# Linear attention's output product: the last two heads' numerators taken through the zero rows of the other heads

## The chip, the cores and the metric

One core of one Trainium2 chip. The metric is the device time of one execution in microseconds; the runs shown give its median. All data is float32; the matrix products of the large stages run in fp32r on operands split into a high and a low half, so that one product of the mathematics is three on the engine (high by high, high by low, low by high).

## The reference, cut to what matters

```python
def _A_ref(x, wqkv, w_phi, wo):          # S = 2048 tokens, D = 640, H = 32 heads of 20
    q, k, v = ...                          # x @ wqkv, by head
    phi_q = concat([softmax(q @ w_phi), softmax(-(q @ w_phi))])   # 40 features a head
    phi_k = ...                            # the same of k
    kv = einsum("bhsf,bhsd->bhfd", phi_k, v)
    z = einsum("bhsf->bhf", phi_k)
    num = einsum("bhqf,bhfd->bhqd", phi_q, kv)
    den = einsum("bhqf,bhf->bhq", phi_q, z)[..., None] + 1e-6
    return (num / den).reshape(B, S, D) @ wo

h = layernorm(x) * (1 + ca) + sa           # sa, ca, ga, sb, cb, gb: six rows made from c
x = x + ga * _A_ref(h, ...)
h = layernorm(x) * (1 + cb) + sb
x = x + gb * (relu(h @ w1 + b1) ** 2 @ w2 + b2)
```

## The kernel before, in words

The tokens are worked in 16 tiles of 128, two tiles a pair `j` (0 to 7). The program has three stretches: K, V and Q with the sums over all tokens; then the division, the numerators and the output product; then the feed-forward part. Only the middle one is touched. There the engines' orders are written out by hand (`manual_schedule`): each of TensorE (PE), VectorE (DVE), ScalarE (ACT) and GpSimd (POOL) takes its instructions as the Python code issues them. SP's order, which holds most loads, comes from a scheduler. The loop `for j in range(NB)` at line 1188 makes eight passes; pass `j` finishes the output product of pair `j` and prepares the numerators of pair `j + 1`.

Names that the text uses:

- 32 heads of 20 are six groups: five of 120 columns (six heads) and a sixth of 40 (the last two heads, called the tail here). `kvd` holds K-by-V of the five as 120 features by two halves of 64 columns, of which 60 are the head columns and 4 are zero; `kv5` holds the tail's, 80 by 40, three times beside each other.
- `e_prod`, `e_recip`, `e_scale` (DVE and POOL, lines 877 to 914): denominators, and the exponentials `ezb` scaled by them.
- `tr_e(j, gs)` (line 916): TensorE transposes `ezb` into a bank `te`, ACT copies the bank to `ept` (lines 927 and 929). The banks `te`, `numa` and `numb` come in turn from three buffers, the six `ept` of a pair from five.
- `num(j)` (line 931): for each of the five groups two fp32 products, 64 columns each, beside each other in the array, to `numa`, `numb` and the first half of `numc`; the tail's two products (64 and 56 columns: its 40 rows three times) go to the second half of `numc`.
- `num_hi` and `num_lo` (lines 952 and 956): ACT copies a high half to `ot`; DVE subtracts to the low half (`lo`, line 89). For pairs 0 and 1 the subtraction is a product with the negated identity, and ACT copies the low half.
- `do_wo(j, i, h)` (line 972): the output product of token tile `2j + i`, half `h` of the columns (384 or 256): 15 products for the five groups and a 16th for the tail, whose three kinds stand in one 120-row operand; then ACT copies `pwo` to `at`, and after the second half a DMA on ACT's queue stores `at` to `a1`.
- `plus_x(j)`: POOL's accumulating DMAs add x to `a1`.
- `prep_wo(g)` (line 489): loads the rows of `wo` for a group into `rwo`, 60 to each half, the four rows between set to zero, and splits them.
- `p_load`, `p_hi`, `p_lo` (lines 992 to 1049): the feed-forward weights, loaded by SP into `rw` or `rawt` and split by ACT and DVE into `w`.

Of the kernel before, what the change touches and what calls it, by code (L numbers as in the profile page):

```python
# [11 lines left out]
AF = mybir.ActivationFunctionType  # L12
# [3 lines left out]
P = 128  # L16
# [21 lines left out]
PLAIN = 2  # L38
DEALT = range(NT // 2)
DIRECT = 2  # L40
LAST = 3
W_AT = (
    *range(21),
# [9 lines left out]
def kernel(  # L53
# [67 lines left out]
    def feat(tag, name):  # L121
        return row(tag, name)[:, :512].rearrange("p (s n) -> p s n", s=2)
# [366 lines left out]
    def prep_wo(g, ga_b):  # L489
        o, n = GR[g]  # L490
        t = row("s1", f"rwo{g}")
        m = P
        if g < 5:
            nc.gpsimd.memset(t, 0.0)
            for c in range(2):
                nc.sync.dma_start(t[64 * c : 64 * c + 60], wo[o + 60 * c : o + 60 * c + 60])
        else:
            m = 3 * n
            for i in range(3):
                nc.sync.dma_start(t[i * n : i * n + n], wo[o : o + n])  # L500
        w = wslot(f"wo{g}")
        WO[g] = w
        with tc.issue_after(newest(ET_.DVE)):
            nc.vector.tensor_tensor(t[:m], t[:m], ga_b[:m], op=ALU.mult)
        nc.scalar.activation(w[:m, 0], t[:m], AF.Copy)
        lo(w[:m, 1], t[:m], w[:m, 0])
        if g == 5:
            nc.gpsimd.dma_start(w[2 * n : m, 0], w[2 * n : m, 1])
# [303 lines left out]
    zb = tok2("w", "zb")  # L812
    kvtile = tok2("w", "kvd")
    kv_t = flat(kvtile)
    kvd = kv_t[:120, :640].rearrange("p (g n) -> p g n", n=P)
    kv5 = kv_t[:80, 640:760]
    def make_z():
        at = [(c, b) for b in range(2) for c in range(2)]
        ps = {}
        for c, b in at:  # L820
            r, a, n = slice(64 * c, 64 * c + 64), 480 * b, ((480, 200), (480, 120))[c][b]
            p = ps[c, b] = tp("z") if len(ps) == 3 else bank(f"z{c}_{b}")
            nc.tensor.matmul(p[:, :n], ident[r, 64 * c + 60 : 64 * c + 61].to_broadcast([64, P]),
                             kvs[r, a : a + n], start=True, stop=True)
# [75 lines left out]
    def e_scale(t):  # L900
# [12 lines left out]
            dn[:, :, 30:, None].to_broadcast([P, 2, 2, DH]), op=ALU.mult  # L913
        )

    def tr_e(j, gs):
        for g in gs:
            o, n = GR[g]
            p = bank(f"te{j}_{g}")
            t = EPT[j, g] = feat("s4", f"ept{j}_{g}")  # L920
            for i in range(2):
                for c in range(2 if g < 5 else 1):
                    a = c * 256 + i * P
                    b, m = (2 * o + 120 * c, 120) if g < 5 else (1200, 80)
                    nc.tensor.transpose(p[:m, a : a + P], EU[2 * j + i][:, b : b + m], ident)
            if g < 5:
                nc.scalar.activation(t[:120], p[:120].rearrange("p (s n) -> p s n", s=2), AF.Copy)
            else:
                nc.scalar.activation(t[:80, 0], p[:80, :256], AF.Copy)

    def num(j):
        OT[j] = ht(f"ot{j}", j)
        ps = [bank(f"numa{j}"), bank(f"numb{j}"), tp(f"numc{j}")]
        for g in range(5):
            for c in range(2):
                mm(ps[g // 2][64 * c : 64 * c + 64, (g % 2) * 256 : (g % 2) * 256 + 256],
                   [(kvd[:, g, 64 * c : 64 * c + 64], EPT[j, g][:120, c])], first=(g % 2 == 0), last=False, skip=True)
        for a, b in ((0, 64), (64, 120)):
            mm(ps[2][a:b, 256:], [(kv5[:, a:b], EPT[j, 5][:80, 0])], first=False, last=False, skip=True)
        NUM[j] = ps  # L940
        OT[j, 5] = row("s3", f"ot5_{j}")[:, 80:336].bitcast(F32R)

    NUM = {}
# [1 line left out]
    def num_parts(j):  # L945
        ps, parts = NUM[j], []
        for b, g in ((0, 2), (1, 2), (2, 1)):
            t = OT[j][:, 2 * b : 2 * b + g]
            parts.append((ps[b][:, : 256 * g].rearrange("p (g n) -> p g n", n=256), t[:, :, 0], t[:, :, 1]))
        return parts + [(ps[2][:120, 256:], OT[j, 5][:120], OT[j, 5][:120])]  # L950

    def num_hi(j):
        for src, hi, _ in num_parts(j):
# [15 lines left out]

    PWO, AT = {}, {}  # L970

    def do_wo(j, i, h, a=0, b=16):
        t = 2 * j + i
        if h == 0 and a == 0:
            PWO[t] = pj(f"pwo{t}")
            AT[t] = row("s2", f"at{t}")
        s = slice(i * P, (i + 1) * P)
        cs_, n = slice(*CUT[h]), CUT[h][1] - CUT[h][0]
        terms = []
        for g in range(5):  # L980
            w, o = WO[g], OT[j]
            terms += three(o[:, g, 0, s], o[:, g, 1, s], w[:, 0, cs_], w[:, 1, cs_])
        terms.append((OT[j, 5][:120, s], WO[5][:120, 0, cs_]))
        mm(PWO[t][h][:, :n], terms[a:b], first=(a == 0), last=(b == 16))
        if b == 16:
            nc.scalar.activation(AT[t][:, cs_], PWO[t][h][:, :n], AF.Copy)
            if h:
                nc.scalar.dma_start(A1[t], AT[t])
# [199 lines left out]
    for j in range(NB):  # L1188
        nxt = j + 1 < NB
        b, c = 2 * j + 5, 2 * j + 6  # L1190
        te_at = (0, 1) if 0 < j < 6 else (1, 2)
        if j == 4:
            load_x1(0)
            load_dealt(0)
        if j < 5:
            p_load()
        if j != 5:
            e_prod(b)
        e_recip(b - 1)
        e_scale(b - 1)  # L1200
        if j == 6:
            mod_sum(5, gate_b)
        if j == 5:
            q_chain(KEPT + 3, False)
        load_e(b + 2)
        def te(at):
            for i, gs in enumerate((range(3), (3, 4, 5) if te_at[0] == 0 else (5, 3, 4))):
                if nxt and te_at[i] == at:
                    tr_e(j + 1, gs)

        do_wo(j, 0, 0)
        te(0)
        if j == 5:
            exps(EQ[KEPT + 3])
            q_sums(KEPT + 3)
            e_prod(b)
        do_wo(j, 0, 1)
        if j == 7:
            t2(0, 0)
            t2(0, 1)  # L1220
        te(1)
        if j == 4:
            ln0 = ln_dealt(0)
            next(ln0)
            next(ln0)
        if j == 6:
            next(ln0)
            turn(0, 0)
            turn(0, 1)
        if j == 2:  # L1230
            exps(EQ[KEPT + 1])
        if j in SUMS:
            q_sums(KEPT + SUMS[j])
        e_prod(c)
        if j != 5:
            e_recip(b)
            e_scale(b)
        do_wo(j, 1, 0)
        if j == 7:
            t2(0, 2)  # L1240
            t2(0, 3)
        te(2)
        if nxt:
            num(j + 1)
            num_hi(j + 1)
        do_wo(j, 1, 1, 0, 8)
        if j == 7:
            t2(0, 4)
            p = tp("gbt")[:NC, :P]
            nc.tensor.transpose(p, gate_b, ident)  # L1250
            nc.scalar.activation(gate_r, p, AF.Copy)
            nc.sync.dma_start(GD[1], gate_r)
            nc.sync.dma_start(gb_b, GD[1].rearrange("c p -> (c p)")[None, :].to_broadcast([P, D]))
        if not nxt:
            do_wo(j, 1, 1, 8, 16)
        if nxt:
            do_wo(j, 1, 1, 8, 11)
            num_lo(j + 1)
            do_wo(j, 1, 1, 11, 16)
# [12 lines left out]
        if j == 4:  # L1272
            next(ln0)
            next(ln0)
            next(ln0)
        if j == 5:
            next(ln0)
        if j == 5:
            p_lo(4)
            p_load(4)  # L1280
        if j == 6:
            p_hi(4)
            p_lo(5)
            p_load(3)
        if j == 7:
            p_load(2)
# [485 lines left out]
```

## Time and profile before

| | |
|---|---|
| median of 3 runs | 756.28 us (756.26 to 756.48) |
| span of the profiled execution, first to last instruction | 754.9 us |
| TensorE busy, granted clock | 749.6 us (99%), 1.000 |
| VectorE, ScalarE, GpSimd busy | 607.5, 458.8, 170.4 us |
| HBM read and written | 100.94 and 29.89 MB |

The profile is of one execution; its times are counted from its first instruction. The profiled execution has no time of its own beside the span; the runs' median is 1.4 us above it. Busy times of TensorE count pipelined products with modelled ends, so a busy engine can still be late. A row of a timeline is: start, us, engine, line, operation, output and input, count, and in brackets the idle time ahead with what ended it. In a chain a row is: start, us, engine, tile, line, count. "ACTq" and "SPq" are the engines' queues issuing DMAs. The middle stretch lies at about 266 to 389 us.

### The profile page before, as it was taken

To read this page: it belongs to the slowest core of one execution; us is meant where nothing else is said; L and a number is where in the kernel's file an instruction comes from. 1 tells how busy PE (TensorE), PEld (TensorE's weight loads), DVE (VectorE), ACT (ScalarE), POOL (GpSimd) and SP (SyncE) were. 2 spreads that over 40 slices of the span, in tenths; PEclk is the share of its full clock that TensorE was granted. 3 is DMA by queue.
4 is the path that set the end of the run, shared out by engine and by line. 5 is a ranking of instruction groups with operands and counts; after the bars stand their busy time and mean duration, and the time that the engine had idled before them with its cause. 6 is when DMAs were issued, how large, how long until landed. Compare 5 with 4: busy or idle time off the path is not lost.

```text
span 754.9 us, 15404 instructions
## 1 busy us (share of the span) xinstructions
PE 749.6 (99%) x5888; PEld 731.9 (97%) x5888; DVE 607.5 (80%) x1123; ACT 458.8 (61%) x1060; POOL 170.4 (23%) x365
## 2 busy tenths in 40 slices
PE   9999999999999999999999999999999999999998
PEld 9999999999999998998899999999999999999997
DVE  6598987988999899999755768787777776777766
ACT  5767666677863355556677757485574756647431
POOL 3001101011200237646303030132221313213110
PEclk9999999999999999999999999999999999999999
DMA  9811431342432264664777475897677767667461
GB/s 324 336 39 80 155 96 70 106 139 103 138 105 93 71 190 142 143 153 124 173 204 218 121 216 215 278 326 204 185 213 204 205 196 212 191 181 208 132 188 36
DMA packets 58931, 126.70 MB, mean 168 GB/s; under 512 B 7452, under 2 KB 16417, under 8 KB 58857
## 3 DMA queue, kind: packets, MB, share of 16 engines
q1 hardware_dynamic: 38706, 79.41, 32.1%
q0 software_dynamic: 17568, 41.00, 22.0%
q10 hardware_dynamic: 2583, 5.30, 1.9%
q8 instruction: 46, 0.75, 0.5%
q14 instruction: 28, 0.23, 0.1%
HBM read 100.94 MB, written 29.89 MB: 173 GB/s over the span
## 4 chain that ended last, share of the span: by engine, by line
PE 86%; DVE 11%; POOL 1%; issue 1%; ACT 0%; DVEq 0%; POOLq 0%
PE up L79 24%; PE acc L79 18%; PE pk L79 9%; PE pv L79 9%; PE pq L79 8%; PE acc3x L79 5%; PE pwo L79 3%; PE kvp L455 3%; DVE dn L883 3%; DVE scr L881 2%; DVE ezb L905 2%; PE foldk L281 1%; PE ta L363 1%; DVE ot L89 1%; POOL dn L889 1%; PE foldq L281 1%
## 5 line engine op out<-in xcount | busy, mean ns | idle before, releaser
L79 PE MATMUL up<-h,w 128*128 128x256 f32 x1640 | 204.4, 276 | 0.1
L79 PEld LDWEIGHTS up<-h,w 128*128 128x128 f32 x1640 | 196.4, 188 | 0.5 <-DVE h L89 0.3
L1321 ACT ACTIVATE ft<-up,b_t 128x256 f32<-128x256 f32 x104 | 48.9, 471 | 96.0 <-PE up L79 95.6
L79 PE MATMUL acc<-w,ra 128*128 128x384 f32 x452 | 97.5, 335 | 0.0
L79 PE MATMUL pwo<-wo,ot 128*128 128x256 f32 (+3 forms) x512 | 79.9, 311 | 0.4 <-DVE ot L89 0.4
L1322 DVE TENSOR_TENSOR ft<-ft 128x256 f32<-128x256 f32 x104 | 43.8, 421 | 43.0 <-ACT ft L1321 41.4
L79 PEld LDWEIGHTS pwo<-wo,ot 128*128 128x128 f32 (+1 forms) x512 | 74.3, 188 | 3.5 <-issue 2.7
L79 PE MATMUL pq<-wq,hT 128*128 128x384 f32 (+1 forms) x480 | 75.1, 311 | 0.0
L79 PEld LDWEIGHTS acc<-w,ra 128*128 128x128 f32 x452 | 72.7, 188 | 0.9 <-DVE ra L89 0.6
L79 PE MATMUL pk<-wk,hT 128*128 128x384 f32 (+1 forms) x480 | 72.7, 308 | 0.0
L79 PE MATMUL pv<-wv,hT 128*128 128x384 f32 (+1 forms) x480 | 71.6, 306 | 0.0
L79 PEld LDWEIGHTS pq<-wq,hT 128*128 128x128 f32 x480 | 71.0, 188 | 0.6 <-issue 0.2
L79 PEld LDWEIGHTS pk<-wk,hT 128*128 128x128 f32 x480 | 70.5, 188 | 0.4 <-issue 0.2
L79 PEld LDWEIGHTS pv<-wv,hT 128*128 128x128 f32 x480 | 70.0, 188 | 0.0
L89 DVE TENSOR_TENSOR ra<-ft,ra 128x384 fp32r<-128x384 f32 (+2 forms) x86 | 36.8, 449 | 32.7 <-ACT ra L1345 19.4
L1431 POOL DMA_DIRECT2D ring_a<-td_a x34 | 18.5, 544 | 117.1 <-PE acc L79 103.7
L1345 ACT ACTIVATE ra<-ft 128x384 fp32r<-128x384 f32 x48 | 25.2, 526 | 28.5 <-DVE ft L1322 22.4
L79 PE MATMUL acc3x<-w,ra 128*128 128x256 f32 x231 | 39.5, 278 | 0.0
L79 PEld LDWEIGHTS acc3x<-w,ra 128*128 128x128 f32 x231 | 37.2, 188 | 0.0
L1336 DVE TENSOR_TENSOR ft<-ft 128x128 f32<-128x128 f32 x136 | 33.4, 286 | 1.2
L446 DVE TENSOR_REDUCE sk<-ek 128x64 f32<-128x1280 f32 x16 | 23.7, 1483 | 12.4 <-ACT ek L441 10.8
L889 POOL TENSOR_TENSOR dn<-dn,rs_q 128x32 f32<-128x32 f32 x32 | 19.9, 622 | 59.0 <-DVE dn L883 58.7
(264 smaller groups left out, 1458.2 us busy)
## 6 DMA issues: line engine op xcount, KB each, us to landing
ring_c<-td_c POOLq DMA_DIRECT2D x34, 384.0 KB, 4.1
ring_a<-td_a POOLq DMA_DIRECT2D x34, 384.0 KB, 3.5
ring_b<-td_b POOLq DMA_DIRECT2D x34, 256.0 KB, 3.5
esp<-eq SPq DMA_DIRECT2D x12, 640.0 KB, 3.2
el<-esp SPq DMA_DIRECT2D x12, 640.0 KB, 4.4
rw<-in_w SPq DMA_DIRECT2D x23, 320.0 KB, 3.5
wm<-in_w_mod SPq DMA_DIRECT2D x20, 320.0 KB, 3.7
xb<-in_x SPq DMA_DIRECT2D x8, 640.0 KB, 4.0
```

The lines of the kernel that those rows point to most:

```text
L79: nc.tensor.matmul(o, a, b, start=first and i == 0, stop=last and i == len(terms) - 1, skip_group_check=skip,)
L89: (eng or nc.vector).tensor_tensor(out_lo, full, hi.bitcast(F32), op=ALU.subtract)
L281: nc.tensor.matmul(p[g // 3][:, (g % 3) * 120 : (g % 3) * 120 + n], r, bd_t[:120, g * 120 : g * 120 + n], start=True, stop=True,)
L446: nc.vector.tensor_reduce(s, heads(flat(e)), axis=AX.X, op=ALU.add)
L455: nc.tensor.matmul(kvp[g // 4][64 * c : 64 * c + 64, a : a + 2 * n].rearrange("p (s n) -> p s n", s=2), v[:, u], e[:, :, o : o + n], start ...
L883: nc.vector.tensor_reduce(dn.rearrange("p s h -> p (s h)"), heads(z), axis=AX.X, op=ALU.add)
L889: nc.gpsimd.tensor_tensor(dn[:, s], dn[:, s], rs[:, 1 - s], op=ALU.mult)
L1321: nc.scalar.activation(r, p, AF.Relu, bias=b1_t[:, f : f + 1])
L1322: nc.vector.tensor_tensor(r, r, r, op=ALU.mult)
L1336: nc.vector.tensor_tensor(t[:, o], t[:, a], t[:, b], op=op)
L1345: nc.scalar.activation(a[:, 0, :3], t[:, :3], AF.Copy)
L1431: nc.gpsimd.dma_start(RING[j, n, r], TD[n][r].bitcast(F32R))
```

## The change

From pair 1 on (`JOINED = 1`) the tail has no rows of its own in `ot`. `kvd` gets eight more rows, 120 to 127, which hold ones so that row 120 + 4c + r goes to column 60 + r of half c of each group. `ept` of the five groups gets eight rows of the tail's numerators in its partitions 120 to 127, and the 128-row products of `num` write them to the four columns of each half that were zero. `wo`'s rows 600 to 639 are loaded to the matching rows of the five `rwo` tiles, which POOL no longer clears.

To have the tail's numerators early, `num_tail` does them by one 40-column product ahead of `num`, in the middle of a half of `do_wo`: behind 8 of the 15 products of (0, 1) in passes 1 to 5, behind 6 of (1, 0) in passes 0 and 6. ACT copies them out of `numc`, and five DMAs on ACT's queue bring eight rows each, once for each half, to the five `ept`. For that the sixth group is transposed first: `tr_e` takes groups 5, 0, 1 and then 2, 3, 4, where it took 0, 1, 2 and then 3, 4, 5 (5, 3, 4 in passes 0 and 6). `do_wo` of pairs 1 to 7 has 15 products, `num` 10 where it had 12, and the tail's high and low half go from ACT and DVE. Pair 0 is as before, with the tail's 16th product.

```diff
+JOINED = 1
...
 def prep_wo(g, ga_b):
-            nc.gpsimd.memset(t, 0.0)
             for c in range(2):
+                e = 600 + 8 * g + 4 * c
                 nc.sync.dma_start(t[64 * c : 64 * c + 60], wo[o + 60 * c : o + 60 * c + 60])
+                nc.sync.dma_start(t[64 * c + 60 : 64 * c + 64], wo[e : e + 4])
...
-    kvd = kv_t[:120, :640].rearrange("p (g n) -> p g n", n=P)
+    kvd = kv_t[:, :640].rearrange("p (g n) -> p g n", n=P)
+    nc.gpsimd.memset(kv_t[96:, :640], 0.0)
+    nc.gpsimd.tensor_copy(
+        kv_t[96:, :640].rearrange("p (g c n) -> p g c n", g=5, c=2)[:, :, :, 60:],
+        ident[96:, None, 120:].rearrange("p g (c r) -> p g c r", c=2).to_broadcast([32, 5, 2, 4]),
+    )
...
+    def num_tail(j):
+        NTP[j] = tp(f"numc{j}")
+        mm(NTP[j][:40, 256:], [(kv5[:, :40], EPT[j, 5][:80, 0])], skip=True)
+        t = row("s3", f"ot5_{j}")[:40, :256]
+        nc.scalar.activation(t, NTP[j][:40, 256:], AF.Copy)
+        place_e(j, *range(5))
+        for g in range(5):
+            nc.scalar.dma_start(EPT[j, g][120:], t[8 * g : 8 * g + 8, None, :].to_broadcast([8, 2, 256]))
...
 def num(j):
+        joined = j >= JOINED
+        k = P if joined else 120
...
-                   [(kvd[:, g, 64 * c : 64 * c + 64], EPT[j, g][:120, c])], first=(g % 2 == 0), last=False, skip=True)
+                   [(kvd[:k, g, 64 * c : 64 * c + 64], EPT[j, g][:k, c])], first=(g % 2 == 0), last=False, skip=True)
+        NUM[j] = ps
+        if joined:
+            return
...
 def do_wo(j, i, h, a=0, b=None):
-        terms.append((OT[j, 5][:120, s], WO[5][:120, 0, cs_]))
+        if j < JOINED:
+            terms.append((OT[j, 5][:120, s], WO[5][:120, 0, cs_]))
...
-            for i, gs in enumerate((range(3), (3, 4, 5) if te_at[0] == 0 else (5, 3, 4))):
+            for i, gs in enumerate(((5, 0, 1), (2, 3, 4))):
...
-        do_wo(j, 0, 1)
+        do_wo(j, 0, 1, 0, 8)
+        if nxt and te_at[0] == 0:
+            num_tail(j + 1)
+        do_wo(j, 0, 1, 8)
...
-        do_wo(j, 1, 0)
+        do_wo(j, 1, 0, 0, 6)
+        if nxt and te_at[0] == 1:
+            num_tail(j + 1)
+        do_wo(j, 1, 0, 6)
```

ACT's order in pass 6 before, from the store of `a1` of token tile 12 on (the numbers in names are those of buffers; in brackets the semaphores that an instruction waits for):

```order
L988 DMA a_12_216<-at_4548 128x640 [waits DMAHW6_49,Activation_49]
L927 ACTIVATE ept_0_4585<-te_0_4584 120x512 [waits PE_49]
L927 ACTIVATE ept_1_4592<-te_1_4591 120x512 [waits PE_49]
L927 ACTIVATE ept_2_4599<-te_2_4598 120x512 [waits PE_49]
L1146 ACTIVATE xx_4140<-xx_4140,rna_4246 128x160 [waits DMAHW4_49,DMAHW3_49]
L1146 ACTIVATE xx_4140<-xx_4140,rna_4246 128x160 x3
L986 ACTIVATE at_4613<-pwo_0_4611 128x384 [waits DMAHW2_49,PE_49]
L929 ACTIVATE ept_5_4632<-te_5_4631 80x256 [waits PE_49]
L927 ACTIVATE ept_3_4637<-te_3_4636 120x512 [waits PE_49]
L927 ACTIVATE ept_4_4644<-te_4_4643 120x512 [waits PE_49,Activation_49]
```

The same place on ACT now:

```order
L941 ACTIVATE ept_1_4599<-te_1_4598 120x512 [waits PE_49]
L1176 ACTIVATE xx_4146<-xx_4146,rna_4259 128x160 x4
L951 ACTIVATE ot_7_4622<-numc_4620 40x256 [waits PE_49]
L954 DMA ept_0_4592<-ot_7_4622 8x2x256 [waits DMAHW0_49,Activation_49]
L954 DMA ept_1_4599<-ot_7_4622 8x2x256
L954 DMA ept_2_4624<-ot_7_4622 8x2x256 [waits DMAHW7_49,DMAHW2_49]
L954 DMA ept_3_4625<-ot_7_4622 8x2x256 [waits DMAHW3_49]
L954 DMA ept_4_4626<-ot_7_4622 8x2x256 [waits DMAHW4_49]
L1016 ACTIVATE at_4613<-pwo_0_4611 128x384 [waits PE_49]
L941 ACTIVATE ept_2_4624<-te_2_4642 120x512 [waits PE_49]
L941 ACTIVATE ept_3_4625<-te_3_4648 120x512 [waits PE_49]
L941 ACTIVATE ept_4_4626<-te_4_4654 120x512 [waits PE_49]
```

The tail's copy and its five DMAs stand ahead of the `at` copy and of the copies of groups 2, 3 and 4; the copy of group 5 went to the front. SP's loads in the same place of the program, now:

```order
L1132 DMA xx_4146<-a_1_205 32x4x160 [waits DMAHW2_49]
L1038 DMA rawt_4539<-in_w 128x640 [waits DMAHW1_49,DVE_49]
L1041 DMA rawt_4539<-in_w 128x640 [waits DMAHW2_49]
L1038 DMA rw_6_4547<-in_w 128x640 [waits DMAHW3_49,DVE_49,Activation_49]
L1041 DMA rw_2_4708<-in_w 128x640 [waits DMAHW4_49,DVE_49,Activation_49]
L1038 DMA rw_7_4711<-in_w 128x640 [waits DMAHW5_49,DVE_49,Activation_49]
L1041 DMA rw_3_4714<-in_w 128x640 [waits DMAHW7_49,DVE_49]
```

`rw_6` counts on DMAHW3 and `rw_2` on DMAHW4: the DMAs of SP and ACT take eight semaphores in turn, in the order of the program, and each waits for the one that had its semaphore before it.

The copy and DMAs in pass 5, ACT, now (`eq` are the exponentials of the last token tile):

```order
L442 ACTIVATE eq15_2839<-eq15_2839 128x640
L443 ACTIVATE eq15_2839<-eq15_2839 128x640
L951 ACTIVATE ot5_6_4430<-numc6_4428 40x256
L954 DMA ept6_0_4394<-ot5_6_4430 8x2x256
L954 DMA ept6_1_4401<-ot5_6_4430 8x2x256
L954 DMA ept6_2_4432<-ot5_6_4430 8x2x256
L954 DMA ept6_3_4433<-ot5_6_4430 8x2x256
L954 DMA ept6_4_4434<-ot5_6_4430 8x2x256
L1016 ACTIVATE at10_4371<-pwo10_1_4370 128x256
L1018 DMA a1_10_214<-at10_4371 128x640
L941 ACTIVATE ept6_2_4432<-te6_2_4449 120x512
```

Before, the `at` copy followed the two exponentials there.

More of the change, by code (lines that the diff above doesn't have):

```diff
@@ L914, in e_scale, with place_e @@
         )
+    def place_e(j, *gs):
+        for g in gs:
+            if (j, g) not in EPT:
+                EPT[j, g] = feat("s4", f"ept{j}_{g}")
     def tr_e(j, gs):
@@ L919, in tr_e @@
             p = bank(f"te{j}_{g}")
-            t = EPT[j, g] = feat("s4", f"ept{j}_{g}")
+            place_e(j, g)
+            t = EPT[j, g]
             for i in range(2):
@@ L929, in tr_e @@
                 nc.scalar.activation(t[:80, 0], p[:80, :256], AF.Copy)
+    NTP = {}
+    def num_tail(j):
[6 more added lines that the diff above has]
+            nc.scalar.dma_start(EPT[j, g][120:], t[8 * g : 8 * g + 8, None, :].to_broadcast([8, 2, 256]))
     def num(j):
         OT[j] = ht(f"ot{j}", j)
-        ps = [bank(f"numa{j}"), bank(f"numb{j}"), tp(f"numc{j}")]
+        joined = j >= JOINED
+        k = P if joined else 120
+        ps = [bank(f"numa{j}"), bank(f"numb{j}"), NTP[j] if joined else tp(f"numc{j}")]
         for g in range(5):
@@ L936, in num @@
                 mm(ps[g // 2][64 * c : 64 * c + 64, (g % 2) * 256 : (g % 2) * 256 + 256],
-                   [(kvd[:, g, 64 * c : 64 * c + 64], EPT[j, g][:120, c])], first=(g % 2 == 0), last=False, skip=True)
+                   [(kvd[:k, g, 64 * c : 64 * c + 64], EPT[j, g][:k, c])], first=(g % 2 == 0), last=False, skip=True)
+        NUM[j] = ps
+        if joined:
+            return
         for a, b in ((0, 64), (64, 120)):
             mm(ps[2][a:b, 256:], [(kv5[:, a:b], EPT[j, 5][:80, 0])], first=False, last=False, skip=True)
-        NUM[j] = ps
         OT[j, 5] = row("s3", f"ot5_{j}")[:, 80:336].bitcast(F32R)
@@ L949, in num_parts @@
             parts.append((ps[b][:, : 256 * g].rearrange("p (g n) -> p g n", n=256), t[:, :, 0], t[:, :, 1]))
-        return parts + [(ps[2][:120, 256:], OT[j, 5][:120], OT[j, 5][:120])]
+        return parts if j >= JOINED else parts + [(ps[2][:120, 256:], OT[j, 5][:120], OT[j, 5][:120])]
     def num_hi(j):
@@ L970, with do_wo @@
     PWO, AT = {}, {}
-    def do_wo(j, i, h, a=0, b=16):
+    def do_wo(j, i, h, a=0, b=None):
         t = 2 * j + i
@@ L982, in do_wo @@
             terms += three(o[:, g, 0, s], o[:, g, 1, s], w[:, 0, cs_], w[:, 1, cs_])
-        terms.append((OT[j, 5][:120, s], WO[5][:120, 0, cs_]))
-        mm(PWO[t][h][:, :n], terms[a:b], first=(a == 0), last=(b == 16))
-        if b == 16:
+        if j < JOINED:
+            terms.append((OT[j, 5][:120, s], WO[5][:120, 0, cs_]))
+        mm(PWO[t][h][:, :n], terms[a:b], first=(a == 0), last=(b is None))
+        if b is None:
             nc.scalar.activation(AT[t][:, cs_], PWO[t][h][:, :n], AF.Copy)
@@ L1254 @@
         if not nxt:
-            do_wo(j, 1, 1, 8, 16)
+            do_wo(j, 1, 1, 8)
         if nxt:
@@ L1258 @@
             num_lo(j + 1)
-            do_wo(j, 1, 1, 11, 16)
+            do_wo(j, 1, 1, 11)
         if j == 5:
```

## The prediction

> **What bounds the kernel now.** I read the page first (engine totals, then the chain that ended last), then the chain in order of time through the stage that the change touches, then the timelines of ACT, DVE and SP there.
>
> ```profile
> PE 749.6 (99%) x5888; PEld 731.9 (97%) x5888; DVE 607.5 (80%) x1123; ACT 458.8 (61%) x1060; POOL 170.4 (23%) x365
> PE 86%; DVE 11%; POOL 1%; issue 1%; ACT 0%; DVEq 0%; POOLq 0%
> ```
>
> TensorE is nearly always busy, and 86% of the chain lies on it. The 11% on VectorE is one stretch: in order of time the chain runs on DVE from 266 us until a low half (`ot` of line 89) lets TensorE go on at 348.41, and on TensorE from there.
>
> ```profile
> 347.47 0.29 DVE ezb L910
> 347.76 0.61 DVE ot L89
> ...
> 348.41 2.70 PE pwo L79 x14
> ...
> 352.43 1.89 PE pwo L79 x16
> ...
> 355.42 2.80 PE pwo L79 x16
> 358.22 1.01 PE numa L79 x8
> 359.23 0.86 PE numb L79 x8
> 360.10 0.87 PE numc L79 x8
> 360.96 6.63 PE pwo L79 x48
> ...
> 372.82 1.01 PE numa L79 x8
> ...
> 375.57 9.45 PE pwo L79 x64
> 385.04 0.49 ACT at L986
> ...
> 388.38 0.44 DVE h L89
> ...
> 388.86 3.90 PE up L79 x32
> ```
>
> So two things decide: how early DVE finishes pass 4's share (348.41), and how long TensorE takes from there to the copy at 385.04, behind which ACT builds the first `h` of the feed-forward part. What is gained or lost by then is carried to the end, because TensorE has no gap after it. Pass j is one turn of the loop at line 1188.
>
> **TensorE.** A half of 384 columns takes 2.80/16 = 0.175 us a product, one of 256 takes 1.89/16 = 0.118. Passes 1 to 7 each lose two of either: 2 x (0.175 + 0.118) = 0.59 us, 4.1 in all. The tail's numerator is not saved but moved: numc's block, half of which is the tail's two products, takes 0.87, no more than numb's 0.86, so the tail is 0.43 and stays two fp32 passes when one product of 40 columns does it alone. It now stands between 128-column products. What that switch costs no row shows directly; numa, which follows such products, takes 1.01 where numb takes 0.86, so entering costs 0.15, and the 48 products behind num take 6.63 where 1.89 + 2.80 + 1.89 = 6.58, so leaving costs 0.05. Bounds 0 and 0.2 for each tail; I take 0.2, the nearer form (few columns, fp32), and below nothing is excluded because no work goes with it. Net 0.39 us off each of passes 1 to 6, 0.59 off pass 7, and pass 0 pays 0.2. The negated product of pass 0 that goes is one more 0.1.
>
> [...]
>
> **VectorE.** The last two heads' low half goes from passes 1 to 6.
>
> ```profile
> 361.95 0.73 DVE L89 TENSOR_TENSOR ot<-numc,ot 128x256 fp32r<-128x256 f32 x2
> 362.61 0.33 DVE L896 RECIPROCAL dd<-dd 128x32 f32<-128x32 f32 x1
> ```
>
> Two such subtractions take 362.61 - 361.95 = 0.66, so one is 0.33. Three of them lie ahead of 347.76 on the chain: TensorE can go on 1.0 us earlier there. TensorE itself is not late then: it waits in this place now, and its own passes get shorter.
>
> **ScalarE and the small DMAs.** The copy of the tail replaces the old copy of the last heads. New are five DMA issues in each of seven passes, on ACT's queue, ahead of copies that TensorE needs. Pass 5, now:
>
> ```profile
> 355.03 0.74 ACT L441 ACTIVATE eq<-eq 128x640 f32<-128x640 f32 x1 [1.86 <-DVE eq L438]
> 355.68 0.72 ACT L442 ACTIVATE eq<-eq 128x640 f32<-128x640 f32 x1
> 356.30 0.36 ACT L986 ACTIVATE at<-pwo 128x256 f32<-128x256 f32 x1
> 356.70 0.33 ACTq L988 DMA_DIRECT2D a<-at  x1
> 357.07 1.08 ACT L927 ACTIVATE ept<-te 120x512 f32<-120x512 f32 x2 [0.40 <-ACT at L986]
> ```
>
> An issue holds ACT 357.07 - 356.70 = 0.37, and one that waits for a copy starts 0.40 behind it. No DMA of 16 rows stands here; a queue's issue takes 0.33 for 128 rows, and I use 0.40 with its semaphore (bounds 0.3 and 0.5). The exponentials wait for DVE, which by then has lost four subtractions, 1.3 us. So: tail copy at 356.30 - 1.3 = 355.0, first issue 355.4, the fifth done 357.4, then the `at` copy and its DMA 0.77, and the copy of ept2 starts at 358.15 and ends at 358.75. The first num product takes over a bank that this copy must have read (three banks, taken in turn), so num starts at 358.75, not 358.22; without the tail it needs 360.96 - 358.22 - 0.43 = 2.31 and ends at 361.06 against 360.96. The 1.0 us is used up: +0.1. In passes 1 to 4 the same 2 us lie in ACT's waits, and in pass 0, where the tail comes late, num may start 1 us later; DVE decides in all of these and is not reached.
>
> Pass 6 is the place where it goes wrong, and the order of ACT and SP shown with the change is its reason. DMAs of SP and ACT share eight semaphores, dealt in turn; each waits until the DMA that had its semaphore before has landed. The fourth and fifth tail DMA of this pass take over those of the first two `rw` loads, and behind them on ACT stand the copies that num needs.
>
> ```profile
> 360.76 0.68 DVE L89 TENSOR_TENSOR ot<-numa,ot 128x512 fp32r<-128x512 f32 x1
> ...
> 364.79 2.29 DVE L89 TENSOR_TENSOR w<-rw,w 128x640 fp32r<-128x640 f32 x3
> ...
> 365.67 0.33 SPq L1008 DMA_DIRECT2D rw<-in_w  x1
> 366.41 0.33 SPq L1011 DMA_DIRECT2D rw<-in_w  x1
> ...
> 369.87 1.75 ACT L1146 ACTIVATE xx<-xx,rna 128x160 f32<-128x160 f32 x4
> 371.77 0.49 ACT L986 ACTIVATE at<-pwo 128x384 f32<-128x384 f32 x1
> 372.16 0.37 ACT L929 ACTIVATE ept<-te 80x256 f32<-80x256 f32 x1
> ```
>
> The views of the DMA issues, by stretch (last column: us from issue to landing):
>
> ```profile
> rw<-in_w SPq DMA_DIRECT2D x4, 320.0 KB, 10.0
> ...
> rawt<-in_w SPq DMA_DIRECT2D x4, 320.0 KB, 4.6
> ...
> xx<-a SPq DMA_DIRECT2D x2, 80.0 KB, 2.1
> ```
>
> A load of this burst lands 10.0 us after its issue (the middle of those that the view follows), an equal one in a calmer stretch 4.6. The burst's second I estimate at 9.0, near its own row. It is asked for when DVE is through with `w`, behind the low halves of pass 5. These start at 360.4, not 360.76 (num from 358.75, numa 1.01, its high copy 0.6; `e_prod` is through by then), and are 0.33 shorter: 0.7 sooner, asked for at 365.7, landed at 374.7. ACT ends its four `xx` at 369.87 + 1.75 = 371.6, which moves up by 0.3 with TensorE (0.41 less in the three halves since num, 0.1 late) and by 0.2 because the small ept5 is now among the first three copies; the tail copy takes 371.1 to 371.5, three issues go until 372.7, and ACT then stands still for 2 us. Fifth issue 374.7 to 375.1, the `at` copy 0.39, ept2 0.6: num starts at 376.1 and ends 2.31 later, 378.4, against 375.57 now: +2.85. Behind it the half of pass 6 and the two of pass 7's first token tile lose 0.118 + 0.175 + 0.118 = 0.41 ahead of the copy at 385.04. Sum +2.4 on a span of 754.9.
>
> **GpSimd and SP.** Five memsets of 631 ns go from GpSimd, where nobody waits. A memset of 32 rows, a small copy and the two first products of `e_prod` now wait for the last V product instead.
>
> ```profile
> 239.91 8.60 PE pv L79 x60
> 258.46 1.43 POOL dn L889
> L494 POOL MEMSET rwo<- 128x640 f32 x5 | 3.2, 631 | 13.7 <-DVE wm L297 9.5 <-DVE wo L89 4.1
> ```
>
> They have from 248.5 to 258.46 for less than 2 us: nothing, or up to 2 us on the DVE chain if that cover went. SP issues ten more loads of four rows, 3.3 us in all, long before their use: nothing.
>
> **The rivals.**
> - *The loads land soon.* If the burst takes 4.6 us, no semaphore is late: five issues 371.5 to 373.5, `at`, ept2 until 374.5, num until 376.85: +1.3 - 0.4 = +0.9, 757.2. Against it: the 10.0 row; for it: the accumulating DMAs of the burst start earlier too.
> - *Faster: ACT's 2 us never reach TensorE.* Then 1.0 at 348.41, 0.39 in passes 5 and 6 and 0.29 of pass 7 ahead of ACT's last copies come through: -2.1, 754.2. In pass 5 ept2 would have to be copied by 356.8, so five issues would have to cost under 0.1 us together. Every issue row says 0.33 apiece.
> - *Slower still: the tail DMA itself lands late*, 5 us after its issue in that burst instead of 2.1 as the two `xx` loads. It decides when over 3.1. Then group 4's product starts at 379.7 and num ends at 380.1: +4.5 - 0.4, 760.4. [...]
>
> **How the numbers follow.** The runs' median, 756.28, stands 1.4 above the profiled span; I add the difference to it: 756.28 + 2.4 = 758.7. Chances: likeliest 0.55, still slower 0.13, loads soon 0.24, faster 0.08. A measurement here can tell 0.2%, 1.5 us, from no change. "Loads soon" is no change, and of the likeliest a little falls either side: slower 0.66, same 0.25, faster 0.09. The range leaves out most of the faster case and the far end of the late landing: 756.0 to 760.6.
>
> **What would show it.** In the profile after: 28 fewer products on `pwo`; `ot` from numc once, not twice, on DVE; five DMA issues near 0.4 us behind the tail's copy on ACT; TensorE waiting in front of num in pass 5 by about half a microsecond more and in pass 6 by 3, the latter with ACT waiting for a DMA ahead of its last issues. No gap on ACT there would make the sum wrong by 1.5 us; no gap on TensorE would make it wrong in sign.

## The result, and the profile after

| | before | after |
|---|---|---|
| median of the runs, us | 756.26 (5 runs, 755.47 to 756.48) | 769.9 (5 runs, 765.8 to 771.42) |
| ratio, 95% interval | | 1.017 (1.0148 to 1.0192) |
| profiled execution, us | 756.28 | 765.8 |
| its span, us | 754.9 | 764.1 |
| mean granted clock, runs in order of time | 1.000 in the profile | 0.999 (765.8), 0.996 (768.57), 0.994 (769.9), 0.993 (769.98), 0.995 (771.42) |

The change makes the kernel 1.7% slower: 13.6 us by the medians, but 9.2 us of span in the profiled execution, which was the fastest of the five. The forecast was slower by 2.4 us.

The page of the profile after, engine totals and the chain that ended last, by engine:

```profile
PE 747.6 (98%) x5845; PEld 726.5 (95%) x5845; DVE 606.1 (79%) x1117; ACT 457.5 (60%) x1059; POOL 166.3 (22%) x362
PE 88%; ACT 3%; ACTq 3%; DVE 2%; DMA 2%; issue 1%; POOL 0%; POOLq 0%
```

TensorE has 2.0 us less to do and the span is 9.2 longer. In the chain VectorE's 11% have shrunk to 2%, and an entry that was not there before has come: ACTq, the time in which ScalarE's sequencer issues DMAs, 3% of 764 us.

The chain in order of time shows what took VectorE's place. This is pass 1, from the tail's product to the numerators:

```profile
295.28 0.57 PE numc L80 x2
...
295.88 0.39 ACT ot L951
...
296.28 0.71 ACTq L954
...
297.03 0.69 ACTq L954
...
297.77 0.70 ACTq L954
...
298.50 0.70 ACTq L954
...
299.24 0.70 ACTq L954
...
299.98 0.39 ACT at L1016
...
300.39 0.32 ACTq L1018
...
300.76 0.61 ACT ept L941
...
301.41 1.08 PE numa L80 x8
```

L954 is the tail's DMA, L1018 the store of `at`. One tail issue holds ACT 0.70 us where the store takes 0.32, and with the step between two the five take 3.7 us. The copy of `ept` that numa waits for stands behind them. Numa starts at 301.41; before, at 298.85.

ACT's timeline in passes 5 and 6 (in brackets: idle before, and what ended it):

```profile
359.23 3.65 ACTq L954 DMA_DIRECT2D ept<-ot  x5
362.92 0.38 ACT L1016 ACTIVATE at<-pwo 128x256 f32<-128x256 f32 x1 [3.72 <-DMA ept<-ot]
...
376.71 0.37 ACT L951 ACTIVATE ot<-numc 40x256 f32<-40x256 f32 x1
377.11 3.71 ACTq L954 DMA_DIRECT2D ept<-ot  x5
380.86 0.49 ACT L1016 ACTIVATE at<-pwo 128x384 f32<-128x384 f32 x1 [3.78 <-DMA ept<-ot]
381.25 1.57 ACT L941 ACTIVATE ept<-te 120x512 f32<-120x512 f32 x3
```

The view names a DMA as releaser of the `at` copy, but the five issues fill the gap from end to end: 359.23 + 3.65 is 362.88, and the copy starts at 362.92. ACT was not waiting; its sequencer was at work. In pass 6 the five take 3.71 us, hardly more than in pass 5, so none of them waited long for a semaphore there.

TensorE's timeline in the same two passes:

```profile
364.35 1.08 PE L80 MATMUL numa<-ept,kvd 128*64 128x256 f32 x8 [2.75 <-ACT ept L941]
...
381.99 1.08 PE L80 MATMUL numa<-ept,kvd 128*64 128x256 f32 x8 [3.26 <-DMA ept<-ot]
384.30 5.95 PE L80 MATMUL pwo<-wo,ot 128*128 128x256 f32 x42
```

The gaps in front of the numerators are 2.75 and 3.26 us. The start of numa in each pass, from the timelines, and of the first `up` product, which stands some 2 us ahead of the one that the chain names (e2 to e7 are kernels of the experiments below; in e7 the start of numa's first product of 120 rows):

| pass | 0 | 1 | 2 | 3 | 4 | 5 | 6 | first `up` |
|---|---|---|---|---|---|---|---|---|
| before | 283.42 | 298.85 | 313.48 | 328.15 | 342.78 | 358.15 | 372.76 | 386.81 |
| after | 285.61 | 301.41 | 316.47 | 331.53 | 347.16 | 364.35 | 381.99 | 394.87 |
| no DMAs (e2) | 283.85 | 299.78 | 314.13 | 328.62 | 343.49 | 358.29 | 372.58 | 385.58 |
| three DMAs (e6) | 285.18 | 300.36 | 314.71 | 329.10 | 343.51 | 359.93 | 375.97 | 388.85 |
| DMAs on SP (e3) | 283.73 | 299.80 | 315.19 | 329.54 | 344.00 | 359.53 | 378.09 | 392.55 |
| no DMAs, five products more (e7) | 284.44 | 299.41 | 313.61 | 328.23 | 342.57 | 357.96 | 372.31 | 385.30 |

Each row is one execution, and they part a little before the change bears on them: the first numerators of all, those of pair 0, start at 269.56 us before, 268.83 after, 269.17 in e2 and 269.87 in e6.

Against the kernel without DMAs, after is late by 1.8 us in pass 0 (2.1, counted from the numerators of pair 0), by 3.7 in pass 4, by 6.1 in pass 5 and by 9.4 in pass 6. Nothing is given back later.

### The profile page after: what moved, and what is told of

It reads as the page before. It is cut to its first block, busy times and chain, and to the rows that moved or that the text cites. A ratio compares the mean times of both kernels' runs of the same rounds, so it can differ in the third digit from the quotient of the medians.

```text
span 764.1 us, 15391 instructions
## 1 busy us (share of the span) xinstructions
PE 747.6 (98%) x5845; PEld 726.5 (95%) x5845; DVE 606.1 (79%) x1117; ACT 457.5 (60%) x1059; POOL 166.3 (22%) x362
## 4 chain that ended last, share of the span: by engine, by line
PE 88%; ACT 3%; ACTq 3%; DVE 2%; DMA 2%; issue 1%; POOL 0%; POOLq 0%
PE up L80 23%; PE acc L80 17%; PE pq L80 9%; PE pk L80 9%; PE pv L80 9%; PE acc3x L80 5%; PE pwo L80 5%; PE kvp L456 3%; ACTq L954 3%; PE te L939 1%; DMA ring_a<-td_a 1%; PE numa L80 1%; PE ta L364 1%; PE foldk L282 1%; DMA ept<-ot 1%
## 5 line engine op out<-in xcount | busy, mean ns | idle before, releaser
L80 PE MATMUL pwo<-wo,ot 128*128 128x384 f32 (+1 forms) x484 | 77.4, 313 | 0.0
L80 PEld LDWEIGHTS pwo<-wo,ot 128*128 128x128 f32 x484 | 70.5, 188 | 5.6 <-issue 5.5
L1016 ACT ACTIVATE at<-pwo 128x384 f32<-128x384 f32 (+1 forms) x32 | 13.9, 436 | 41.9 <-DMA ept<-ot 26.7
```

The source lines that it names most:

```text
L80: nc.tensor.matmul(o, a, b, start=first and i == 0, stop=last and i == len(terms) - 1, skip_group_check=skip,)
```

## The experiments

The theory (A) was that ACT's time for issuing is the cause. The rivals were the landing of the DMAs (B), and the new order of the transposes or the tail product itself (C). The spread of the runs needed a theory of its own. In the diffs, `-` is the changed kernel.

**e1: nobody waits for the DMAs.**

```diff
-        k = P if joined else 120
+        k = 120
```

> The five DMAs of each tail are issued on ACT as in the changed kernel, but the numerator products read only the 120 rows of the large heads, so nothing waits for the DMAs to land (the last two heads' numerators of passes 1 to 7 are left out of the output). Theory A, it is the time that ACT spends on issuing (0.70 us and a step of 0.04 for each, 3.7 us a pass) that holds back the copies of te2 to te4: nothing changes, 764 to 771 us like the changed kernel, first numerator product of pass 6 between 381.5 and 382.0 us (in the changed kernel 381.99). Rival B, it is the landing of the DMAs that the numerators wait for (the waits give it 3.3 us in pass 6): the time falls by at least 3 us, and the first numerator product of pass 6 comes before 379 us.

Measured: 770.15 us (4 runs, 768.34 to 771.94), ratio to before 1.0191 (1.0174 to 1.0208). The numerators of pass 6 started at 384.38, later than either theory said, with a gap of 3.16 us put to ACT's copy. The 2.4 us more than in the profile after are all there by pass 1: this execution is 0.77 us late in pass 0 (286.38), and half clock behind that pass's gap adds 1.7 (see e5); from pass 1 on the distance stays between 2.4 and 2.5. Taking the landing away gives nothing: B falls as the cause in the changed kernel. The first DMA of pass 6 does land late there, at 381.85, but ACT's copies of `ept` behind the issues last until 382.82.

**e2: no DMAs.**

```diff
-        k = P if joined else 120
+        k = 120
...
-        place_e(j, *range(5))
-        for g in range(5):
-            nc.scalar.dma_start(EPT[j, g][120:], t[8 * g : 8 * g + 8, None, :].to_broadcast([8, 2, 256]))
```

> The changed kernel without its five DMAs a pass: the tail product and ACT's copy of it stay, the numerators read 120 rows, the new order of the transposes and the 15 products stay (the last two heads' numerators of passes 1 to 7 are left out of the output). Theory A (issues): with 26 us of ACT's issuing gone the copies of te2 to te4 are early enough again, the first numerator product of pass 6 comes at 370.5 to 372.8 us, and the kernel takes 753.5 to 755.5 us, the forecast's sum without its term for ACT being 754.2. Rival C, the order of the transposes, the tail product's switch or its copy cost TensorE the time: still above 760 us. In both the granted clock tells whether it follows TensorE's gaps: 0.999 or more if theory A holds and the gaps are gone.

Measured: 754.48 us (10 runs, 754.02 to 755.66), ratio 0.9977 (0.9968 to 0.9986), granted clock 0.999 or 1.000 in every run. TensorE's timeline in passes 5 and 6 has no gap in front of the numerators:

```profile
358.29 1.08 PE L80 MATMUL numa<-ept,kvd 120*64 120x256 f32 x8
...
372.58 1.08 PE L80 MATMUL numa<-ept,kvd 120*64 120x256 f32 x8
```

Everything else of the change but the eight rows of the tail's numerators is in this kernel, so C falls, and the five DMAs are the whole loss: 15.4 us by the medians. e1, which reads the same 120 rows, differs from it by the DMAs alone, and by 15.7 us. What is left of the change is a gain of 1.9 us.

**e3: the DMAs on SP.**

```diff
-            nc.scalar.dma_start(EPT[j, g][120:], t[8 * g : 8 * g + 8, None, :].to_broadcast([8, 2, 256]))
+            nc.sync.dma_start(EPT[j, g][120:], t[8 * g : 8 * g + 8, None, :].to_broadcast([8, 2, 256]))
```

> The same five DMAs issued on SP. ACT is freed of 3.7 us a pass, the DMAs must still land before the numerators. Theory A: the copies of te2 to te4 are early again; what is left is the landing. If an issue holds SP 0.70 us as it holds ACT, the DMAs for the first bank go out by 1.5 us behind the tail's copy and land some 2 us later, about 1 us after the point where the numerators of the kernel before began (298.85 in pass 1), so 757 to 761 us. Rival B (landing): the numerators wait as long as in the changed kernel, 764 us or more.

Measured: 763.36 us (4 runs, 762.14 to 764.14), ratio 1.0092 (1.0077 to 1.0107). It lies between the two expectations. SP's timeline in pass 6:

```profile
373.05 3.85 SPq L954 DMA_DIRECT2D ept<-ot  x5
```

and the chain there:

```profile
373.05 4.91 DMA ept<-ot
...
378.09 1.94 PE numa L80 x7
```

An issue holds SP about as long as ACT: the five take 3.85 us here and 3.71 on ACT. With ACT free, the landing comes to light: up to pass 4 the kernel is within 1.1 us of the one without DMAs, and in pass 6 the first tail DMA lands 4.91 us after its issue began, in the burst of loads.

**e9: on SP, and nobody waits.** The edits of e1 and e3 together.

```diff
-        k = P if joined else 120
+        k = 120
...
-            nc.scalar.dma_start(EPT[j, g][120:], t[8 * g : 8 * g + 8, None, :].to_broadcast([8, 2, 256]))
+            nc.sync.dma_start(EPT[j, g][120:], t[8 * g : 8 * g + 8, None, :].to_broadcast([8, 2, 256]))
```

> The five DMAs of a pass issued on SP and not waited for (the numerators read 120 rows, so the last two heads' numerators of passes 1 to 7 are left out of the output): the fourth corner of the square whose other three are ACT and waited for (the changed kernel, 769.9 us), ACT and not waited for (770.2) and SP and waited for (763.4). Theory A with the landing behind it: neither ACT's time nor the landing is in the way, 754 to 756 us like the kernel without DMAs (754.5), clock 0.999 or more; then all of the 8.9 us that the SP kernel loses against that is the wait for the landing. Rival T, the transfers themselves or SP's queue (its loads of the weights stand behind the issues) cost time: 758 us or more.

Measured: 755.89 us (10 runs, 755.37 to 756.62), ratio 0.9992 (0.9983 to 1.0001), no gap of 0.8 us on TensorE: theory A. That closes the square:

| | waited for | not waited for |
|---|---|---|
| issued on ACT | 769.9 | 770.15 |
| issued on SP | 763.36 | 755.89 |
| no DMAs | | 754.48 |

The landing costs 7.5 us when SP issues, 1.7 of them in the profiled execution half clock behind the one long gap (see e5), and nothing when ACT does, because ACT's issues and the copies behind them then last as long. The 1.4 us between the last two may be the transfers or SP's queue; no run parts these.

**e4: plain rows.** ACT copies the tail twice side by side, and each DMA takes eight rows of 512.

```diff
-        nc.scalar.activation(t, NTP[j][:40, 256:], AF.Copy)
+        nc.scalar.activation(
+            t.rearrange("p (c n) -> p c n", c=2), NTP[j][:40, None, 256:].to_broadcast([40, 2, 256]), AF.Copy
+        )
...
-            nc.scalar.dma_start(EPT[j, g][120:], t[8 * g : 8 * g + 8, None, :].to_broadcast([8, 2, 256]))
+            nc.scalar.dma_start(EPT[j, g][120:], t[8 * g : 8 * g + 8].rearrange("p (c n) -> p c n", c=2))
```

> ACT copies the tail twice side by side, and each DMA moves 8 plain rows of 512 numbers instead of 8 rows of 2 x 256 from one copy; still on ACT, same bytes. Theory A1, the issue is dear because of its form (8 x 2 x 256 with a repeated source): an issue falls from 0.70 us to the 0.33 of the store of at, 1.8 us a pass less on ACT, and the kernel takes 756 to 761 us. Rival A2, an issue to these rows costs 0.7 us in any form: no change, 764 to 771 us.

Measured: 767.67 us (4 runs, 766.04 to 770.09), ratio 1.0153 (1.0132 to 1.0174). The issues by line (ns, minimum, median, maximum):

```profile
L956 ACTq DMA_DIRECT2D ept<-ot x35: 631/632/1633, 281.7 to 383.1; - x35
```

0.63 us in place of 0.70: the repeated source costs a tenth, not half. A1 falls.

**e8: the price of an issue by form.** Eleven DMAs on ACT behind its last work (its total time says nothing), `bb` and `gb_b` being tiles in SBUF and `in_x` an input in DRAM. In the views `a` is the DRAM buffer `A1`; in the diff `a` and `b` are short for `bb` and `gb_b`.

```diff
     last_downs(NB - 1)
+    a, b = bb, gb_b
+    for o, i in (
+        (b[120:, :512], a[:8, :512]),
+        (b[:8, :512], a[:8, :512]),
+        (b[64:104, :512], a[:40, :512]),
+        (b[104:120, :512], a[:16, :512]),
+        (b[20:21, :512], a[:1, :512]),
+        (b[:, 512:], a[:, :128]),
+        (A1[0][:8, :512], a[:8, :512]),
+        (A1[1], a),
+        (b[10:18, :512], x[:8, :512]),
+        (b[32:40, :512].rearrange("p (c n) -> p c n", c=2), a[:8, None, :256].to_broadcast([8, 2, 256])),
+        (b[40:48, :128], a[:8, :128]),
+    ):
+        nc.scalar.dma_start(o, i)
```

> The changed kernel with eleven DMAs of other forms issued on ACT behind its last work: the price of an issue by form. Theory F, the price goes with where the rows lie (8 rows of SBUF into 8 rows of SBUF 0.63 to 0.70, whatever the columns, and 0.33 for 128 rows into DRAM): 8x512 within SBUF 0.6 or more, 8x512 into DRAM 0.33 or less. Rival N, it goes with the number of rows or bytes: 1 row, 8 rows and 40 rows within SBUF differ by more than 0.2 us from each other, and SBUF to DRAM costs the same as SBUF to SBUF at one size.

The groups of that line (ns, minimum, median, maximum):

```profile
L1763 ACTq DMA_DIRECT2D gb_b<-bb x8: 580/670/809, 763.6 to 770.0; - x8
...
L1763 ACTq DMA_DIRECT2D a<-bb x2: 352/402/452, 767.8 to 768.3; - x2
L1763 ACTq DMA_DIRECT2D gb_b<-in_x x1: 337/337/337, 768.7 to 768.7; - x1
```

From SBUF into SBUF an issue takes 0.58 to 0.81 us, one by one in the order of the list: 0.71, 0.65, 0.76 (40 rows), 0.58 (16), 0.60 (one row), 0.60 (128 rows), then 0.81 for the repeated source and 0.69 for eight short rows. Into DRAM it takes 0.45 (eight rows) and 0.35 (128), out of DRAM 0.34. The number of rows and bytes does not order these eleven; where both ends lie does. F holds but for 0.45 where it said 0.33; N falls, though 40 rows against 16 do differ by 0.18. Each form was issued once. The ends are not all there is, either: ACT's first DMA, 120 rows out of DRAM, is as dear already in the kernel before:

```profile
0.80 0.67 ACTq L207 DMA_DIRECT2D bdc<-in_bd  x1
```

**e6: three issues instead of five.** The prediction gave ACT 2.0 us a pass; three issues are 2.2.

```diff
-        k = P if joined else 120
+        k = 120
...
-        for g in range(5):
+        for g in range(3):
             nc.scalar.dma_start(EPT[j, g][120:], t[8 * g : 8 * g + 8, None, :].to_broadcast([8, 2, 256]))
```

> Three DMAs a pass on ACT in place of five, not waited for, and the numerators read 120 rows (the last two heads' numerators of passes 1 to 7 are left out of the output). Three issues take 2.2 us of ACT, about the 2.0 us that the prediction put on all five. Theory S, only the size of an issue was wrong and the cover that the prediction saw for 2 us in passes 0 to 4 is there: 755 to 758 us, TensorE waiting in front of the numerators only in passes 5 and 6. Rival V, the cover was not there either: about three fifths of the way from 754.5 us (no DMA) to 770.2 us (five), 762 to 765 us.

Measured: 758.81 us (5 runs, 758.36 to 759.01), ratio 1.0035 (1.0022 to 1.0048). TensorE's timeline has just two gaps of 0.8 us or more:

```profile
359.93 1.08 PE L80 MATMUL numa<-ept,kvd 120*64 120x256 f32 x8 [1.53 <-ACT ept L941]
...
375.97 1.08 PE L80 MATMUL numa<-ept,kvd 120*64 120x256 f32 x8 [1.65 <-ACT ept L941]
```

By the table this kernel is 1.3 us behind e2 in pass 0 (0.7 of which it was behind already at the numerators of pair 0), 0.0 in pass 4, 1.6 in pass 5 and 3.4 in pass 6. So 2.2 us are covered up to pass 4, as S says, and cost 1.6 to 1.8 in each of passes 5 and 6; its time is 0.8 above S's upper end and far below V.

**e5: the gaps filled with idle products.** This is about the spread of the runs. The profiles of e1, e3, e4 and e8 show the granted clock falling to half behind some gaps. TensorE in e3, window by window of 1 us (busy PE, PEld, DVE, ACT, POOL; then the clock, the share of the DMA engines, GB/s):

```profile
377.00:378.00 1.00, 0.00 (x0) 0.00 (x0) 0.00 (x0) 0.00 (x0) 0.55 (x1) 0.98 0.29 62
378.00:379.00 1.00, 0.91 (x5) 0.60 (x7) 0.00 (x0) 0.00 (x0) 0.00 (x0) 0.50 0.95 98
379.00:380.00 1.00, 1.00 (x8) 0.67 (x6) 0.00 (x0) 0.00 (x0) 0.00 (x0) 0.50 0.90 158
380.00:381.00 1.00, 1.00 (x8) 0.62 (x6) 0.27 (x1) 0.60 (x1) 0.00 (x0) 0.50 0.45 78
381.00:382.00 1.00, 1.00 (x8) 0.42 (x5) 0.42 (x1) 0.33 (x1) 0.00 (x0) 0.81 0.00 0
```

Behind the gap of 3.46 us that ended at 378.09 the clock stands at 0.50 for 3.4 us, which loses 3 x 0.5 + 0.19 = 1.7 us of work.

```diff
         if nxt:
+            for _ in range({0: 12, 4: 5, 5: 18, 6: 22}.get(j, 0)):
+                mm(PWO[2 * j + 1][1][:, :256], [(OT[j][:, 0, 0, P:], WO[0][:, 0, 384:])], skip=True)
             num(j + 1)
```

> The changed kernel with products that nobody reads put ahead of the numerators where TensorE stood still longest: 12 in pass 0, 5 in pass 4, 18 in pass 5, 22 in pass 6, of 128 x 256 at about 0.118 us, which is 1.4, 0.6, 2.1 and 2.6 us against gaps of 2.03, 1.09, 2.75 and 3.26 us in the profiled changed kernel. They are overwritten by the next real product of their bank, so the result is the same and the waits for ACT end when they ended. Theory G, a gap of two microseconds or more is answered at times by 3.4 us of half clock (0.50 in windows of 1 us behind the gap in three of the profiles, costing 1.7 us each), and that is what parts 765.8 from 771.4 us in the runs of the changed kernel: with the gaps filled every run has a granted clock of 0.998 or more and takes 764.5 to 767.5 us. Rival P, the clock falls for another reason, such as where the transfers lie: clocks of 0.993 to 0.997 and 768 to 772 us stay.

Measured: 766.59 us (4 runs, 766.19 to 766.85), clock 0.999 or 1.000 in all. TensorE's timeline in pass 6:

```profile
379.40 2.75 PE L80 MATMUL pwo<-wo,ot 128*128 128x256 f32 x22
382.84 1.08 PE L80 MATMUL numa<-ept,kvd 128*64 128x256 f32 x8 [0.69 <-ACT ept L941]
```

The numerators start no earlier (382.84 against 381.99), and yet the median falls by 3.3 us and the spread from 5.6 to 0.7 us. G holds: without the long gaps no run shows the lower clock. So of the 13.6 us about 3.3 are clock, an estimate from the medians of five and four runs, and the rest is standing still less what the products save.

**e7: the same sum without DMAs.** The last two heads go straight into the three banks by five products a pass, weights in `kv5p` (zero but for 8 of 128 columns), operands F32R. It replaces the tail product, its copy and the DMAs.

```diff
+        if joined:
+            for g in (0, 1, 4, 2, 3):
+                mm(ps[g // 2][:, (g % 2) * 256 : (g % 2) * 256 + 256],
+                   [(KVP[0][:, g], EPT[j, 5][:80, 0].bitcast(F32R))], first=(g % 2 == 0), last=False, skip=True)
...
-        do_wo(j, 0, 1, 0, 8)
-        if nxt and te_at[0] == 0:
-            num_tail(j + 1)
-        do_wo(j, 0, 1, 8)
+        do_wo(j, 0, 1)
```

> No DMAs and no tail product: the last two heads' part is added into the three banks by five products of 80 rows and 128 columns a pass, whose weights are zero but in the eight columns of the zero rows, in one rounded pass (F32R) each. Theory A: five products of 256 columns at 0.11 to 0.12 us, 0.6 us a pass, stand for the 0.43 us of the tail's two products before and the 0.14 us of the switch, ACT loses the copy of the tail and every issue, TensorE keeps the 0.59 us a pass of the 28 products: 753.5 to 755.5 us like the kernel without DMAs, clock 0.999 or more. Rival W, the products wait for the second bank's copy and the fifth transpose's buffer is held until they are done: TensorE stands still for 0.5 us a pass and the kernel takes 756 to 759 us.

Measured: 755.0 us (11 runs, 754.31 to 755.73), ratio 0.9983 (0.9974 to 0.9992). TensorE's timeline in pass 1:

```profile
298.73 0.40 PE L80 MATMUL numa<-ept,kv5p 80*128 80x256 f32 x2
298.96 0.28 PE L80 MATMUL numc<-ept,kv5p 80*128 80x256 f32 x1
299.08 0.40 PE L80 MATMUL numb<-ept,kv5p 80*128 80x256 f32 x2
299.41 1.08 PE L80 MATMUL numa<-ept,kvd 120*64 120x256 f32 x8
```

The five take 299.41 - 298.73 = 0.68 us (up to 0.92 in pass 6), and there is no gap ahead of numa. By the medians this kernel is 1.3 us faster than before, and 15 us faster than the changed kernel.

**e10: pass 0 too.** The edits of e7, with `JOINED = 0` and the weights made ahead of the first numerators.

```diff
-JOINED = 1
+JOINED = 0
```

> The kernel with five products of 80 rows in place of DMAs, now in pass 0's numerators too, so that all eight passes have 15 products. By the terms that held in the other seven passes, 0.59 us of products saved, 0.43 of the tail's products saved and 0.6 spent: 0.4 us less than the 755.0 us with seven passes, 754.2 to 755.2 us. Rival: the weights must now be ready before the first numerators, ACT's extra copy and the first pass's wait for DVE take the gain back: 755.0 to 756.5 us.

Measured: 754.65 us (11 runs, 753.86 to 755.73), ratio 0.9976 (0.9967 to 0.9985): 1.9 us faster than before by the medians. That it is also faster than e7 is likely, but the two intervals overlap.

## Why the prediction was wrong

The sign was right, and the size was not: 2.4 us forecast, 13.6 measured, outside the range.

**The step that failed** is the price of an issue: "a queue's issue takes 0.33 for 128 rows, and I use 0.40 with its semaphore (bounds 0.3 and 0.5)". It was 0.70 and 0.04 for the step, 3.7 us a pass instead of 2.0. The rows behind 0.33 to 0.37 are moves between SBUF and DRAM; the new DMA stays within SBUF, and e8 prices that at 0.58 to 0.81 for anything from one row to 128. The bounds were taken from two rows of another kind, and no row of the kernel before was of this kind. Nor was it so that "every issue row says 0.33 apiece": the 0.67 shown with e8 is a row of the kernel before. Beside the DMA an issue is not small here: one takes 0.70 us on ACT, where `359.84 2.02 DMA ept<-ot` in e3's chain has such a DMA landed 2.02 us after its issue begins: a third of it. Five together take 3.71 us, more than three quarters of the 4.74 to the first one's landing in pass 6.

**The cover** was sized rightly and then exceeded. The prediction held that in passes 1 to 4 "the same 2 us lie in ACT's waits", and in pass 0 up to 1 us is lost. With 2.2 us (e6) pass 0 lost 0.6 us against e2, counted from the numerators of pair 0, and by pass 4 all of it was made up. With 3.7 us, pass 4 is reached 3.7 us late. The bound named ahead, DVE until 348.41, then no longer decides alone: in passes 0 to 3 the chain after runs from the tail's product through ACT's issues to numa, and in passes 4 and 5 it comes from DVE (334.16 to 338.38 and 350.56 to 357.54) to the tail's copy and goes through the same issues.

**Pass 5**: forecast +0.1 with the 1.0 us of DVE's earlier end and 0.4 of shorter products used up, a loss of 1.5 against no DMAs. With three issues it is 1.6. With five, after loses 2.4 us in this pass alone.

**Pass 6**: forecast +2.85 by two issues that wait for the semaphores of the `rw` loads. That did not come: the five issues took 3.71 us without a stop. ACT was so late by then that the loads had landed (375.29 and 377.77, against issues at 379.38 and 380.12). So this wait was hidden, not refuted. In e9, where SP issues on time, it is there: in pass 6 the five issues take 4.78 us, and 1.0 of them is a wait for an `rw` load (a timeline row of SP, then what SP waited for):

```profile
370.40 4.78 SPq L954 DMA_DIRECT2D ept<-ot  x5
...
SPq L954 <- DMA rw<-in_w: 1.0, 1, 1.0
```

What the changed kernel has is the third rival's mechanism, a late landing:

```profile
377.11 4.74 DMA ept<-ot
381.86 0.14 issue
381.99 1.08 PE numa L80 x8
```

4.74 us, where the rival said 5, but beside ACT's copies, which e1 shows to end no sooner (a gap of 3.16 us there, 3.26 here); it costs next to nothing here and decides only where SP issues. The chance of 0.13 for "still slower" was my estimate: no row of the kernel before showed how a DMA of few rows fares among these loads. In e3 the first of the five lands 4.91 us after its issue began in this pass, where one of pass 5 took 2.02.

**TensorE** came out as worked out, **VectorE** only in part. The `pwo` products went from 512 to 484, 28 fewer (before, then after), and DVE subtracts from numc once:

```profile
L79 PE MATMUL pwo<-wo,ot 128*128 128x256 f32 (+3 forms) x512 | 79.9, 311 | 0.4 <-DVE ot L89 0.4
...
L80 PE MATMUL pwo<-wo,ot 128*128 128x384 f32 (+1 forms) x484 | 77.4, 313 | 0.0
```

```profile
304.64 0.41 DVE L90 TENSOR_TENSOR ot<-numc,ot 128x256 fp32r<-128x256 f32 x1
```

The tail's product is followed by the next `pwo` product after 0.55 us:

```profile
375.02 0.62 PE L80 MATMUL numc<-ept,kvd 80*40 80x256 f32 x2
375.57 1.85 PE L80 MATMUL pwo<-wo,ot 128*128 128x384 f32 x9
```

That is 0.43 and a switch of 0.12, inside its bounds of 0 and 0.2. The sum without ACT was -2.1 us, and e2, which is that kernel, measured -1.9. GpSimd's and SP's new work was held to cost nothing, which fits that sum; no run takes it alone. That the two sums agree so closely is partly luck. Of the 1.0 us that VectorE was to give at 348.41, e2's profiled execution has 0.14, because VectorE stands still there for a load of `el`, a wait that the profile before does not have (a row of DVE's timeline, then of the chain):

```profile
286.76 1.49 DVE L889 TENSOR_TENSOR scr<-el,zb 128x1280 f32<-128x1280 f32 x1 [1.16 <-DMA el<-esp]
...
348.27 2.54 PE pwo L80 x13
```

e10, without that wait, has the product at 347.46, 0.95 us earlier than before. Why the load comes late in e2 no run shows.

**What the sum had no term for** is the clock. "What is gained or lost by then is carried to the end" counts a gap once; a gap of 2 us or more was at times paid again by 1.7 us of half clock, about 3.3 us in the median run. The three issues of e6, with gaps up to 1.65 us, kept 1.000 in all runs.

The first signs named ahead were met (28 products, one subtraction, issues behind the tail's copy). "Near 0.4 us" and "in pass 5 by about half a microsecond more" were two that failed, by 0.70 and 2.75, and both point at the same term. TensorE's wait of 3 us in pass 6 came too, 3.26, but by luck: the reason given for it, ACT waiting for a DMA ahead of its last issues, did not.

## What to carry to other kernels

Price a DMA on the engine that issues it, by a row of the same kind with the same ends, and count every issue as work of that engine ahead of whatever stands behind it in its order; a row of another kind of transfer is no bound for it (in e8 0.58 to 0.81 us within SBUF, 0.34 to 0.45 between SBUF and DRAM). Where several small transfers feed an engine that decides, ask whether that engine can do the move itself: five products of 0.68 to 0.92 us a pass together replaced five DMAs that held ACT for 3.7 us. And price a gap on TensorE of 2 us or more at more than its length: behind six of the twelve such gaps below stood 3.4 us of half clock, which loses 1.7 us each time.

## What the runs showed that was not expected

- An issue from SBUF to SBUF takes 0.58 to 0.85 us on ACT for 1 to 128 rows, and 0.69 to 0.87 on SP for eight (e3), but for single ones of 1.63 (e4) and 1.11 (e9); between SBUF and DRAM e8 has 0.34 to 0.45, and the kernel before one of 0.67. What makes an issue within SBUF dear no run shows.
- Over the profiles of after, e1, e3, e4 and e8, TensorE had twelve gaps of 2.03 to 3.46 us; six were followed by 3.4 us at a granted clock of 0.50, the shortest of these six being 2.03 us (e1, pass 0), and the changed kernel's own profiled execution had three such gaps and none of it. Gaps of 1.89 us and less were never followed by it. The same gap brings it in one execution and not in another: the 2.03 us of pass 0 did in e1 and did not in the changed kernel. What decides it no run shows.
